# Repeated moving columns in two small TensorE products of a convolution and mixture-of-experts kernel, and another order of the logits products

## The chip, the cores and the metric

The kernel runs on one core of one Trainium2 chip. The metric is device time in microseconds. A profiled execution gives a span, from the first to the last instruction, and its own time beside it.

## The reference, cut to what matters

Tokens pass a causal convolution of seven taps per head and then a two-level mixture of experts: four groups of four experts, each token going to one expert, weighted by the product of two softmax values.

```python
# x: 8 x 2880 x 192, weight: 8 heads x 7 taps
w = exp(weight - max); w = w / (sum(w) + 1e-9)
out[b, s, h] = sum_k w[h, k] * x_pad[b, s + k, h]          # x for the experts, 23040 x 192
g_logits = x @ w_group                                     # 192 x 4
g_idx = argmax(g_logits); g_w = softmax(g_logits)[g_idx]
e_logits = x @ w_expert[g_idx]                             # 192 x 4 per group
e_idx = argmax(e_logits); e_w = softmax(e_logits)[e_idx]
y = maximum(x @ w1[g_idx, e_idx], 0) @ w2[g_idx, e_idx]    # 192 x 1024, 1024 x 192
out[token] = g_w * e_w * y
```

## The kernel before, in words

The 23040 tokens are cut into 192 blocks of 120 tokens, and the blocks into 18 units of 4, 8 or mostly 12 blocks. `unit` (L364) routes one unit. For each head a band matrix is multiplied with the tokens (L409), and ScalarE copies the result to `xc` (L418). TensorE turns the first 128 channels of a block into `ta` (L428) and the last 64 channels of two blocks into `tb` (L438). `logits` (L442) then multiplies them with the router weights for four blocks at a time: for each pair of blocks one product of `tb` with `wrb` (L448), which holds the weights of the last 64 channels for both blocks in 40 columns, and two products of `ta` with `wr` (L451), 20 columns each, added in PSUM. ScalarE copies 80 columns out to `lg` (L454). All these are f32. VectorE finds the expert and the weight of each token (L483 to L512), the unit's tokens with their weights are written to memory (L514), two small products count tokens per expert (L523, L524), and VectorE works out each token's place in its expert's list.

The list of a unit is itself made by a product. For each block VectorE writes two f16 matrices of zeros and ones, `ohl` with 128 columns and `ohv` with 32 (L549, L557), and TensorE multiplies them, one product per block, all added into 32 columns of one PSUM bank (L570). VectorE turns these into token numbers (L576, L578), and GpSimd scatters them to the table `idtab` (L581).

The experts come in slots of 256 tokens. GpSimd gathers the tokens (L653), TensorE turns them (L666, L667), `hidden` multiplies with the first weights (L684), ScalarE and VectorE split the result into two parts (L689, L690), and `back` multiplies with the second weights (L702, 384 columns; L706, 192 columns). VectorE and ScalarE add and scale the output (L753, L754), and GpSimd scatters it. The weights are loaded by SyncE (L602 to L606) and split on ScalarE and VectorE (L618 to L634); SyncE also loads the tokens for routing (L205, L207) and the lists (L976).

The first portion of slots needs the lists of the first five units, so these are routed first; the other units are routed in steps that are put between the expert products. The order of emission comes from tables of numbers (`UG`, `SK`, `KPRE`) and a rate, and the framework's scheduler then orders each engine's queue by its own estimate of durations. All PSUM comes from three pools of 2 KB banks; a bank holds 512 columns of f32.

Of the kernel before, what the change touches and what calls it, by code (L numbers as in the profile page):

```python
# [15 lines left out]
AF = mybir.ActivationFunctionType  # L16
# [4 lines left out]
P = 128  # L21
BT = 120
UB = 12
QB = 4
# [4 lines left out]
LH = 32  # L29
# [7 lines left out]
def conv_moe_kernel(  # L37
# [10 lines left out]
    nc = tc.nc  # L48
# [26 lines left out]
    NL = G + E  # L75
# [13 lines left out]
    for b in range(B):  # L89
        k = b * NB  # L90
# [84 lines left out]
    idtab = dram.tile([ROWS, 1], I32, name="idtab")  # L175
    tabd = dram.tile([NTAB, 4], I32, name="tabd")
    NVIEW = 12
    idviews = dram_disjoint_views(idtab[:, :], NVIEW)
    outviews = dram_disjoint_views(out, 8)
    nscat = [0]  # L180
# [48 lines left out]
    wr = const.tile([P, 2, NL], F32, name="wr")  # L229
# [16 lines left out]
    def clear_table():  # L246
# [12 lines left out]
        out=tri, in_=ones, pattern=[[1, P]], compare_op=ALU.is_gt, fill=0.0, base=0, channel_multiplier=-1,  # L259
# [12 lines left out]
    for nb in sorted({n for _, n in units}):  # L272
# [35 lines left out]
        out=sel, in_=ident.rearrange("p (e l) -> p e l", e=E), axis=AX.X, op=ALU.add)  # L308
    nc.gpsimd.iota(io[:, 0:1], pattern=[[0, 1]], base=0, channel_multiplier=1)
    nc.vector.tensor_scalar(  # L310
        out=io[:, 1:2], in0=io[:, 0:1], scalar1=LE - 1, scalar2=None, op0=ALU.bitwise_and)
# [6 lines left out]
    for g in range(NSK):  # L318
        nc.sync.dma_start(
            out=skew[0:R, g * HG:(g + 1) * HG],  # L320
            in_=bass.AP(wvd.tensor, wvd.offset + VL - KS - (BT - 1) + g * HG * VL, [[1, R], [VL, HG], [1, VW]]),
# [13 lines left out]
    for h in range(H):  # L335
        nc.scalar.activation(
            out=band[0:R, h], in_=skew[0:R, h, BT - 1::-1], func=AF.Exp, bias=wm[0:R, h:h + 1],
# [5 lines left out]
    wrb = const.tile([P, 2, NL], F32, name="wrb")  # L343
# [20 lines left out]
    def unit(u, pre=None):  # L364
# [4 lines left out]
        def bank(kind=None):  # L369
            if BK and kind and len(unit_banks) > 1:  # L370
                pool, nm = BKS[BK][kind]
                return pool.tile([P, 512], F32, name=nm)
            npool[0] += 1
            pool, nm = unit_banks[npool[0] % len(unit_banks)]
            return pool.tile([P, 512], F32, name=nm)
# [23 lines left out]
        for h in range(H):  # L399
# [8 lines left out]
            for i, (bb, xx) in enumerate(ops):  # L408
                nc.tensor.matmul(  # L409
                    out=ps[0:BT, 0:nb * HC], lhsT=bb[0:R, h, :], rhs=xx[0:R, :, cs],  # L410
                    start=i == 0, stop=i == len(ops) - 1,
# [8 lines left out]
        lg = rt.tile([P, UB, NL], F32, name="lg")[:, 0:nb]  # L420
# [21 lines left out]
        def logits(q):  # L442

            lgp = bank("l")
            ta, tb = parts[q]
            for i in range(QB // 2):
                o = lgp[0:BT, 2 * i * NL:2 * (i + 1) * NL]
                nc.tensor.matmul(  # L448
                    out=o, lhsT=tb[:, i * BT:(i + 1) * BT], rhs=wrb.rearrange("p a n -> p (a n)"), start=True, stop=False)
                for j in range(2):  # L450
                    nc.tensor.matmul(  # L451
                        out=o[:, j * NL:(j + 1) * NL], lhsT=ta[:, (2 * i + j) * BT:(2 * i + j + 1) * BT], rhs=wr[:, 0],
                        start=False, stop=j == 1)
            nc.scalar.activation(  # L454
                out=lg[0:BT, q * QB:(q + 1) * QB], in_=lgp[0:BT, 0:QB * NL].rearrange("p (b n) -> p b n", n=NL), func=AF.Copy)

        ga, gl, rest = gaps(u)
        events = {}
        for q in range(NQ):
            for k, f in ((ga, turn_a), (ga + 1, turn_b), (ga + gl, logits)):  # L460
                events.setdefault(k + 3 * q, []).append((f, q))
# [5 lines left out]
        Q = BT  # L467

        def bc(a, n):
            return a.unsqueeze(len(a.shape)).broadcast_to([*a.shape, n])  # L470
# [15 lines left out]
            out=sc, in0=dd, scalar=0.0, in1=prio[0:Q].unsqueeze(1).broadcast_to([Q, M, EG]),  # L486
# [9 lines left out]
            out=ohx[0:Q], in0=ohv[:, :, 1:NG, :].rearrange("p b g e -> p g e b"),  # L496
# [20 lines left out]
        while any(need <= u and pi not in idps for need, pi in needs.items()):  # L517
# [20 lines left out]
            out=posb[0:Q, 0], in0=pn, scalar1=-(LH - 1) / 2, scalar2=RND, op0=ALU.add, op1=ALU.add)  # L538
        nc.vector.scalar_tensor_tensor(
            out=posb[0:Q, 1], in0=posb[0:Q, 0], scalar=RND, in1=pn, op0=ALU.subtract, op1=ALU.subtract)  # L540

        halves = []
        for b0 in range(0, nb, HB2):
            n = min(HB2, nb - b0)
            ohl = pa.tile([P, HB2, P], F16, name="ohl", bufs=2)
            ohr = rt.tile([P, HB2, LH], F16, name="ohr", bufs=1)
            ohv5 = pa.tile([P, HB2, LH], F16, name="ohv", bufs=2)
            bs = slice(b0, b0 + n)
            nc.vector.tensor_tensor(  # L549
                out=ohl[0:Q, 0:n], in0=iop[0:Q].unsqueeze(1).broadcast_to([Q, n, P]), in1=bc(posb[0:Q, 0, bs], P),  # L550
# [3 lines left out]
                out=ohr[0:Q, 0:n], in0=ior[0:Q].unsqueeze(1).broadcast_to([Q, n, LH]), in1=bc(posb[0:Q, 1, bs], LH),  # L554
# [3 lines left out]
                out=ohv5[0:Q, 0:n], in0=ohr[0:Q, 0:n], in1=bc(vals[0:Q, bs], LH), op=ALU.mult)  # L558
# [8 lines left out]
        pl = bank("l")  # L567
        for b0, n, ohl, ohv5 in halves:
            for k in range(n):
                nc.tensor.matmul(  # L570
                    out=pl[:, 0:LH], lhsT=ohl[0:Q, k], rhs=ohv5[0:Q, k],
                    start=b0 + k == 0, stop=b0 + k == nb - 1,
                )
        lv5 = rt.tile([P, LH], F32, name="lv5", bufs=1)
# [2 lines left out]
            out=lv5, in0=pl[:, 0:LH], scalar1=0.0, scalar2=float(BIG), op0=ALU.is_equal, op1=ALU.mult)  # L577
        nc.vector.scalar_tensor_tensor(  # L578
            out=lsi, in0=pl[:, 0:LH], scalar=float(t0 - 1), in1=lv5, op0=ALU.add, op1=ALU.add)

        nc.gpsimd.indirect_dma_start(  # L581
            out=TABV, out_offset=bass.IndirectOffsetOnAxis(ap=rowi.bitcast(U32), axis=0),
            in_=lsi, in_offset=None,
# [334 lines left out]
    def step():  # L918

        if routed[0] < NU and len(live) < lead[1] and (not live or max(live, key=lambda a: a[0])[1] >= (lead[0] or SK[min(routed[0], len(SK)) - 1])):  # L920
            u = routed[0]
            live.append([u, 0, unit(u, xin0 if u == 0 else None)])
            routed[0] += 1
        if not live:
            return
        done[0] += 1
        cur = live.pop(0)
        cur[1] += 1
        try:
            next(cur[2])  # L930
            live.append(cur)
        except StopIteration:
            pass
# [84 lines left out]
    def tiles(i):  # L1018

        return 1 if plan[i][0] == "tail" and plan[i][1] >= NBIG else 2  # L1020
# [45 lines left out]
    k = 0  # L1066
    while routed[1] < portions[0][0]:
# [5 lines left out]
        for i in [i for i, kk in enumerate(KPRE) if kk == k]:  # L1073
            e, q = divmod(i, 5)
# [29 lines left out]
    for i, (pi, e, s) in enumerate(plan):  # L1104
# [4 lines left out]
        n = tiles(i)  # L1109
        oo = [po.tile([P, 512], F32, name="po") for _ in range(n)]  # L1110
        steps = NF // 2 if n == 2 else 2
        for f2 in range(steps):
# [27 lines left out]
            for q in range(f2, NF // 2, steps):  # L1140
                k = (q + 2) % 4
# [14 lines left out]
    with tc.If(nrare[0] != 0):  # L1156
        nover = nc.values_load(
            flagi[0:1, 0:1], min_val=0, max_val=1, skip_runtime_bounds_check_because=OOB_WHY)
        with tc.For_i(0, nover, 1):
            for u in range(NU):  # L1160
# [10 lines left out]
                    out=gi[:, 0], in0=gi[:, 1], scalar1=VS.bit_length() - 1, scalar2=None, op0=ALU.logical_shift_right)  # L1171
# [4 lines left out]
                    out=ee, in0=eoff[0:BT].unsqueeze(1).broadcast_to([BT, nb, E]),  # L1176
# [3 lines left out]
                    out=ee, in0=ee, in1=ends[0:BT, u].unsqueeze(1).broadcast_to([BT, nb, E]), op=ALU.mult)  # L1180
# [4 lines left out]
                for k in range(nb):  # L1185
                    nc.gpsimd.indirect_dma_start(
                        out=idtab[:, :], out_offset=bass.IndirectOffsetOnAxis(ap=gi[:, 0, k:k + 1].bitcast(U32), axis=0),
                        in_=idw[:, k:k + 1], in_offset=None,
# [48 lines left out]
```

## Time and profile before

| | |
|---|---|
| median of 3 runs | 1164.26 us (1162.6 to 1168.98) |
| the profiled execution | 1170.84 us, span 1169.0 us |
| mean granted TensorE clock | 0.977 of full speed |
| busy share of the span: PE, PEld, DVE, ACT, POOL | 95%, 92%, 69%, 59%, 43% |
| list products L570, in all | 192 |
| rows of logits products L451 and L448, in all | 384 and 192 |

PE is TensorE's matmul stream and PEld its weight loads, which overlap it; DVE is VectorE, ACT ScalarE, POOL GpSimd, SP SyncE. An f32 matmul stands in the trace as two rows, an f16 one as one. A busy time of PE counts modelled ends, so it is not a measure of useful columns; prices are better read from one start to the next. The granted clock is 1.00 or 0.50 in this trace, and it changes at edges 3.41 us apart.

### The profile page before, as it was taken

Reading aid. Unit: us, or ns where it says so; the run is one execution under the profiler, and the core shown is the slowest. Engines: PE = TensorE matmul, PEld = TensorE weight load, DVE = VectorE, ACT = ScalarE, POOL = GpSimd, SP = SyncE. Lnnn points to the kernel's source line nnn. Section 1 sums busy time; section 2 is a strip of 40 time slices with the busy share of each in tenths; the row PEclk is TensorE's granted clock in tenths of the full one; section 3 lists DMA queues with packets and bytes.
Section 4 is the critical chain, followed back from the end, with each engine's and each line's share of the span. In section 5 each row is a group of like instructions: output and inputs, shape, how many; then the busy total and the mean of one; then the engine's idle time right before and its main releaser. Section 6 shows DMA issues by size and latency. Waiting matters only on the chain.

```text
span 1169.0 us, 23803 instructions
## 1 busy us (share of the span) xinstructions
PE 1111.7 (95%) x8468; PEld 1079.3 (92%) x8468; DVE 804.5 (69%) x1668; ACT 690.1 (59%) x1374; POOL 498.2 (43%) x443
## 2 busy tenths in 40 slices
PE   5887999999999999999999999999999999999994
PEld 4766999998999999999999999999999999998984
DVE  4756788887877676666678565656565656688772
ACT  5544677657655555656554555555555656677772
POOL 2103234434434343434344444444444445578771
PEclk8879999999999999999999999999999999999997
DMA  8766699989775654546354574545454545599960
GB/s 228 217 182 178 173 213 230 226 203 268 217 194 143 165 156 118 143 116 170 95 162 95 155 203 128 142 128 141 130 141 128 140 118 167 146 243 266 248 160 19
DMA packets 167212, 195.63 MB, mean 167 GB/s; under 512 B 22500, under 2 KB 144333, under 8 KB 167086
## 3 DMA queue, kind: packets, MB, share of 16 engines
q1 hardware_dynamic: 125006, 140.41, 44.6%
q0 software_dynamic: 18752, 35.85, 10.5%
q10 hardware_dynamic: 23328, 17.80, 6.2%
q8 instruction: 67, 1.10, 0.4%
q14 instruction: 59, 0.48, 0.1%
HBM read 158.79 MB, written 36.58 MB: 167 GB/s over the span
## 4 chain that ended last, share of the span: by engine, by line
PE 79%; DVE 5%; DMA 4%; issue 3%; ACT 3%; another core or an unknown queue 0%; POOL 0%; POOLq 0%; ACTq 0%; DVEq 0%; SPq 0%
PE ph L684 33%; PE po L702 21%; PE po L706 10%; PE pm L409 3%; DMA xg<-xcd,idpt 3%; PE pm L451 2%; PE pm L666 2%; PE pm L667 2%; PE pm L428 1%; PE ph L719 1%; PE pm L448 1%; DVE hl L690 1%; DVE ohl L549 1%; DMA idtab<-lsi,rowi 1%; ACT cw L633 1%
## 5 line engine op out<-in xcount | busy, mean ns | idle before, releaser
L702 PE MATMUL po<-cw,hh 128*128 128x384 f32 x1424 | 443.4, 369 | 5.9 <-DVE ys L754 5.9
L684 PE MATMUL ph<-xa,ah 128*128 128x256 f32 x1424 | 390.2, 296 | 1.9 <-DVE xa L669 1.5
L757 POOL DMA_INDIRECT out<-ys,idp x160 | 167.8, 1049 | 447.4 <-DVE ys L754 348.8
L706 PE MATMUL po<-cw,hl 128*128 128x192 f32 x1424 | 357.3, 251 | 0.0
L690 DVE SCALAR_TENSOR_TENSOR hl<-ph,hh 128x512 fp32r<-128x512 f32 x356 | 241.2, 686 | 163.5 <-ACT hh L689 149.3
L689 ACT ACTIVATE hh<-ph 128x512 fp32r<-128x512 f32 x356 | 210.8, 594 | 205.8 <-PE ph L684 170.2
L702 PEld LDWEIGHTS po<-cw,hh 128*128 128x128 f32 x1424 | 268.6, 189 | 9.7 <-DVE ys L754 7.6
L684 PEld LDWEIGHTS ph<-xa,ah 128*128 128x128 f32 x1424 | 271.0, 190 | 5.0 <-DVE xa L669 1.6
L706 PEld LDWEIGHTS po<-cw,hl 128*128 128x128 f32 x1424 | 272.6, 191 | 1.5
L653 POOL DMA_INDIRECT xg<-xcd,idp x160 | 190.0, 1187 | 62.0 <-issue 29.6
L684 PE MATMUL ph<-xb,bh 128*128 128x256 f32 x712 | 201.9, 284 | 0.3 <-DVE xb L673 0.3
L684 PE MATMUL ph<-xb,bl 128*128 128x256 f32 x712 | 201.8, 283 | 0.0
L684 PE MATMUL ph<-xa,al 128*128 128x256 f32 x712 | 201.3, 283 | 0.0
L684 PEld LDWEIGHTS ph<-xa,al 128*128 128x128 f32 x712 | 136.5, 192 | 2.1
L684 PEld LDWEIGHTS ph<-xb,bl 128*128 128x128 f32 x712 | 136.7, 192 | 0.0
L684 PEld LDWEIGHTS ph<-xb,bh 128*128 128x128 f32 x712 | 136.2, 191 | 0.4 <-DVE xb L673 0.4
L634 DVE TENSOR_TENSOR cw<-rawc,cw 128x768 fp32r<-128x768 f32 x114 | 105.3, 953 | 18.3 <-ACT cw L633 13.7
L619 DVE TENSOR_TENSOR al<-raw,ah 128x1024 fp32r<-128x1024 f32 x57 | 70.5, 1238 | 38.8 <-ACT ah L618 21.6
L754 DVE SCALAR_TENSOR_TENSOR ys<-po,xg,ys 128x192 f32<-128x192 f32 x187 | 76.2, 416 | 23.2 <-ACT ys L753 18.1
L633 ACT ACTIVATE cw<-rawc 128x768 fp32r<-128x768 f32 x114 | 91.0, 837 | 1.8 <-DMA rawc<-in_moe_w 1.4
L672 ACT ACTIVATE xb<-pm 64x256 fp32r<-64x256 f32 x98 | 36.0, 367 | 93.4 <-DVE xa L669 86.2
L753 ACT ACTIVATE ys<-po,xg 128x192 f32<-128x192 f32 x187 | 75.8, 418 | 22.2 <-PE po L706 12.0
(216 smaller groups left out, 1561.0 us busy)
## 6 DMA issues: line engine op xcount, KB each, us to landing
rawc<-in_moe_w SPq DMA_DIRECT2D x114, 384.0 KB
raw<-in_moe_w SPq DMA_DIRECT2D x57, 512.0 KB
raw<-in_moe_w SPq DMA_DIRECT2D x114, 256.0 KB
xcd<-xc ACTq DMA_DIRECT2D x13, 1085.6 KB
xin<-in_x SPq DMA_DIRECT2D x7, 1134.0 KB
xc<-in_moe_w SPq DMA_DIRECT2D x18, 384.0 KB
xin<-in_x SPq DMA_DIRECT2D x6, 1039.5 KB
xin<-in_moe_w SPq DMA_DIRECT2D x9, 512.0 KB
```

The lines of the kernel that those rows point to most:

```text
L619: eng.get(k, nc.vector).tensor_tensor(out=al, in0=ra, in1=ah.bitcast(F32), op=ALU.subtract)
L633: pin(PINW, nc.scalar.activation(out=cw[:, fs, 0, :], in_=rc[k - 2], func=AF.Copy))
L634: eng.get(k, nc.vector).tensor_tensor(out=cw[:, fs, 1, :], in0=rc[k - 2], in1=cw[:, fs, 0, :].bitcast(F32), op=ALU.subtract,)
L653: nc.gpsimd.indirect_dma_start(out=xs[:, t, :], out_offset=None, in_=xcd[0:known, :], in_offset=bass.IndirectOffsetOnAxis(ap=ids[:, t, 0:1 ...
L684: nc.tensor.matmul(out=hp[:, j], lhsT=wgt[:, fs], rhs=xx, start=i == 0, stop=i == len(ops) - 1)
L689: nc.scalar.activation(out=hh, in_=hp, func=AF.Relu)
L690: nc.vector.scalar_tensor_tensor(out=hl, in0=hp, scalar=0.0, in1=hh.bitcast(F32), op0=ALU.max, op1=ALU.subtract,)
L702: nc.tensor.matmul(out=oo[t][:, 0:2 * D], lhsT=hh[:, j, ts], rhs=cw[:, f].rearrange("p a d -> p (a d)"), start=f == 0, stop=False,)
L706: nc.tensor.matmul(out=oo[t][:, 0:D], lhsT=hl[:, j, ts], rhs=cw[:, f, 0, :], start=False, stop=f == NF - 1,)
L753: nc.scalar.activation(out=ys[:, t, :], in_=oo[t][:, D:2 * D], func=AF.Copy, scale=g)
L754: nc.vector.scalar_tensor_tensor(out=ys[:, t, :], in0=oo[t][:, 0:D], scalar=g, in1=ys[:, t, :], op0=ALU.mult, op1=ALU.add,)
L757: nc.gpsimd.indirect_dma_start(out=outviews[nscat[0] % len(outviews)], out_offset=bass.IndirectOffsetOnAxis(ap=ids[:, t, 0:1].bitcast(U32) ...
```

## The change

Two constants are added, `REPL` = 5 and `REPO` = 6. In `logits`, the moving operand `wr` of a `ta` product is read five times over, so that 100 columns are streamed and written instead of 20; each block has its own 100 columns in the bank, 400 for four blocks, and only the first 20 of each are used. The two `ta` products of a pair now come first, and the product of `tb` follows as the third, writing only the 20 used columns of each of the two blocks (40 columns, as before). The first product of the pair starts the accumulation and the third ends it. ScalarE's copy reads the same 80 values, now 100 columns apart. In the list product the moving operand `ohv` is read six times over, 192 columns instead of 32, and VectorE still reads the first 32. Weight loads, the numbers of products and all other code are unchanged, though the scheduler orders some queues anew. Lines behind L177 move by two, behind the logits by up to four.

```diff
+    REPL = 5
+    REPO = 6
...
             for i in range(QB // 2):
-                o = lgp[0:BT, 2 * i * NL:2 * (i + 1) * NL]
-                nc.tensor.matmul(
-                    out=o, lhsT=tb[:, i * BT:(i + 1) * BT], rhs=wrb.rearrange("p a n -> p (a n)"), start=True, stop=False)
+                o = lgp[0:BT, 2 * i * REPL * NL:2 * (i + 1) * REPL * NL].rearrange("p (j n) -> p j n", j=2)
                 for j in range(2):
                     nc.tensor.matmul(
-                        out=o[:, j * NL:(j + 1) * NL], lhsT=ta[:, (2 * i + j) * BT:(2 * i + j + 1) * BT], rhs=wr[:, 0],
-                        start=False, stop=j == 1)
+                        out=o[:, j].rearrange("p (r n) -> p r n", n=NL), lhsT=ta[:, (2 * i + j) * BT:(2 * i + j + 1) * BT],
+                        rhs=wr[:, 0].unsqueeze(1).broadcast_to([P, REPL, NL]), start=j == 0, stop=False)
+                nc.tensor.matmul(
+                    out=o[:, :, 0:NL], lhsT=tb[:, i * BT:(i + 1) * BT], rhs=wrb, start=False, stop=True)
             nc.scalar.activation(
-                out=lg[0:BT, q * QB:(q + 1) * QB], in_=lgp[0:BT, 0:QB * NL].rearrange("p (b n) -> p b n", n=NL), func=AF.Copy)
+                out=lg[0:BT, q * QB:(q + 1) * QB],
+                in_=lgp[0:BT, 0:QB * REPL * NL].rearrange("p (b n) -> p b n", b=QB)[:, :, 0:NL], func=AF.Copy)
...
                 nc.tensor.matmul(
-                    out=pl[:, 0:LH], lhsT=ohl[0:Q, k], rhs=ohv5[0:Q, k],
+                    out=pl[:, 0:REPO * LH].rearrange("p (r n) -> p r n", r=REPO), lhsT=ohl[0:Q, k],
+                    rhs=ohv5[0:Q, k].unsqueeze(1).broadcast_to([Q, REPO, LH]),
                     start=b0 + k == 0, stop=b0 + k == nb - 1,
                 )
```

## The prediction

> **What bounds the kernel now.** I read the page first, then the busy time in five stretches, then the instructions in time where the three changed lines run, and last the granted clock around its drops.
>
> ```profile
> span 1169.0 us, 23803 instructions
> PEclk8879999999999999999999999999999999999997
> 16.32:116.00 99.68, 78.56 (x536) 67.25 (x535) 62.17 (x241) 51.44 (x142) 15.06 (x14) 0.83 0.76 203
> 116.00:640.00 524.00, 516.58 (x4054) 504.36 (x4055) 389.13 (x844) 314.12 (x636) 208.50 (x177) 0.99 0.65 171
> 640.00:1020.00 380.00, 380.00 (x2940) 379.48 (x2939) 241.85 (x387) 215.64 (x392) 168.80 (x157) 1.00 0.50 143
> ```
>
> After the start and the stretch name, the columns are busy us of PE, PEld, DVE, ACT and POOL, then the granted TensorE clock, the DMA share and GB/s. There are two stages that matter. Up to 116 us the first five units are routed before any expert can start: PE is busy 79% of that stretch at a mean clock of 0.83. From 116 us on TensorE is the bound: 516.58 of 524.00 us while the other units are routed between expert matmuls, and 380.00 of 380.00 us when routing is over. So TensorE time added between 116 and 640 us is paid nearly in full, and before 116 us only where it lies on the chain. The two changed products run only up to 621 us.
>
> **The list product.** These are the rows of one unit of 12 blocks and its neighbours (start, us, engine, line, operation, operands, shape, count).
>
> ```profile
> 132.28 0.25 PE L706 MATMUL po<-cw,hl 128*128 128x192 f32 x1
> 132.36 0.36 PE L702 MATMUL po<-cw,hh 128*128 128x384 f32 x1
> 132.56 0.25 PE L706 MATMUL po<-cw,hl 128*128 128x192 f32 x1
> 132.66 0.47 PE L570 MATMUL pm<-ohv,ohl 120*128 120x32 f16 x12
> 132.97 0.42 PE L702 MATMUL po<-cw,hh 128*128 128x384 f32 x1
> 133.23 0.25 PE L706 MATMUL po<-cw,hl 128*128 128x192 f32 x1
> 116.00:640.00 524.00, 5.19 (x132) 4.19 (x132) 0.99 0.65 171
> L570 PEld LDWEIGHTS <-ohl 120*128 120x128 f16 x192 | 7.5, 100 | 10.6 <-issue 4.6 <-DVE ohl L549 3.7 <-DVE ohv L557 1.4
> ```
>
> Durations overlap, so prices are read from start to start. Twelve 32-column products pass in 132.97 - 132.66 = 0.31 us, 0.026 us each. With 192 columns they cannot: an expert product that streams 192 columns holds the engine 0.08 us (132.28 to 132.36) to 0.09 (131.71 to 131.80 below). That is the upper bound. The lower one comes from the band product (next part): 288 columns in two passes cost 0.245 us a row, 0.245 / 576 = 0.43 ns a column, so 192 cost 0.082. I take 0.085, between them. Twelve are then 1.02 us instead of 0.31, 0.71 more. Something comes back: the L702 behind the list now takes 133.23 - 132.97 = 0.26 us, against 132.56 - 132.36 = 0.20 in the stream, because its weight load outlasts a 32-column product; a 192-column one covers those 0.06. That leaves 0.65 us a unit. The stretch row counts 132 list matmuls in the TensorE-bound stage, 11 units: **11 x 0.65 = +7.2 us** (bounds 6.8 with 0.082 and 7.8 with 0.09). Nothing hides it: TensorE is the engine that ends last there.
>
> The Trainium skill (TensorE: Matmul & The Clock Gate, LDWEIGHTS) prices a weight load at its columns / 1.2 GHz; by that rule 128 columns are 107 ns, the load would already be what the list product waits for, 192 columns would fit under it and this term would be zero. [...] The same page (Back-to-back issue gap) gives N / 2.4 + 2.5 ns, 82.5 ns for 192 columns, an estimate that would make this term 6.8.
>
> **The logits product.** At full clock, at half clock, and a product with 96 columns and two passes at half clock:
>
> ```profile
> 131.03 0.57 PE L451 MATMUL pm<-wr,ta 128*120 128x20 f32 x4
> 131.45 0.42 PE L702 MATMUL po<-cw,hh 128*128 128x384 f32 x1
> 131.71 0.25 PE L706 MATMUL po<-cw,hl 128*128 128x192 f32 x1
> 131.80 0.36 PE L702 MATMUL po<-cw,hh 128*128 128x384 f32 x1
> 71.71 0.97 PE L451 MATMUL pm<-wr,ta 128*120 128x20 f32 x4
> 72.51 1.29 PE L409 MATMUL ph<-xin,band 126*120 126x288 f32 x2
> 9.23 0.61 PE L409 MATMUL pm<-xin,band 126*120 126x96 f32 x2
> 9.63 0.61 PE L409 MATMUL po<-xin,band 126*120 126x96 f32 x2
> 78.46 0.65 PE L409 MATMUL ph<-xin,band 126*120 126x288 f32 x2
> 78.95 0.37 PE L438 MATMUL ph<-ident,xc 120*128 120x120 f32 x2
> ```
>
> An f32 product stands as two rows, each with its own load of 120 weight columns. Four 20-column rows take 131.45 - 131.03 = 0.42 us, 0.10 each at full clock; at half clock 72.51 - 71.71 = 0.80, 0.20 each. A 96-column f32 product of the same weight width takes 9.63 - 9.23 = 0.40 for its two rows, 0.20 each, the same price: both wait for the weight load, not for columns. At full clock 100 columns in two passes stream for 200 x 0.43 = 0.085 us (0.245 a row for 288: 78.95 - 78.46 = 0.49 for two), below 0.10. So the logits repeats cost **0**, covered by their own weight loads. Were that cover gone the price would be 0.10 + 0.085; the 96-column rows speak against it. Nothing is taken off for a gain either, since the loads stay. The order of the three products only swaps equal loads, and the copy out of PSUM still reads 80 elements.
>
> ```order
> L448 MATMUL po<-wrb,tb 120x40
> L451 MATMUL po<-wr,ta 120x20 x2
> L448 MATMUL po<-wrb,tb 120x40
> L451 MATMUL po<-wr,ta 120x20 x2
> L409 MATMUL ph<-xin,band 120x192 x2
> L409 MATMUL po<-xin,band 120x192 x2
> ```
>
> That was TensorE before, shortly ahead of the second unit's list product (wr and wrb are the router weights, ta and tb the turned tokens, band the convolution); this is the same place after the change:
>
> ```order
> L411 MATMUL ph<-xin,band 120x192 x2
> L451 MATMUL po<-wr,ta 120x100 x2
> L454 MATMUL po<-wrb,tb 120x2x20
> L451 MATMUL po<-wr,ta 120x100 x2
> L454 MATMUL po<-wrb,tb 120x2x20
> L411 MATMUL po<-xin,band 120x192 x2
> ```
>
> Two band products have moved ahead of the logits. Nearly every such move lies in the routing stage; behind it TensorE's order is the old one but for a few places.
>
> SyncE's queue moves there too. Before, with raw and rawc the weights and xin the tokens:
>
> ```order
> L602 DMA raw<-in_moe_w 128x1024
> L603 DMA raw<-in_moe_w 64x1024
> L207 DMA xin<-in_x 126x8x192
> L604 DMA raw<-in_moe_w 64x1024
> L606 DMA rawc<-in_moe_w 128x4x192 x2
> ```
>
> and after:
>
> ```order
> L606 DMA raw<-in_moe_w 128x1024
> L610 DMA rawc<-in_moe_w 128x4x192 x2
> L209 DMA xin<-in_x 126x8x192
> L607 DMA raw<-in_moe_w 64x1024
> L608 DMA raw<-in_moe_w 64x1024
> ```
>
> The two rawc loads now stand ahead of the sixth unit's tokens, and would hold them back if their buffer came free late; but that unit is not needed for the first portion, so I count 0 and keep 3 us to either side for all reordering before 116 us, less than the one wait of 3.94 us below.
>
> **The routing stage and the clock.** The chain has these list products and this wait, and the windows of the clock gate (edges from its changes, 3.41 us apart) read so:
>
> ```profile
> 70.44 0.20 PE pm L570 x2
> 83.42 0.30 PE pm L570 x6
> 98.54 0.20 PE pm L570 x8
> 101.03 3.94 another core or an unknown queue
> 67.52:70.93 3.41, 2.29 (x25) 2.00 (x24) 1.01 (x7) 1.08 (x4) 0.00 (x0) 1.00 0.99 273
> 70.93:77.76 6.83, 6.83 (x25) 5.63 (x25) 3.35 (x14) 3.01 (x9) 0.97 (x1) 0.50 0.30 74
> 91.41:94.82 3.41, 3.41 (x37) 3.38 (x35) 1.70 (x11) 2.49 (x7) 0.00 (x0) 1.00 0.92 149
> 94.82:98.24 3.42, 3.42 (x36) 3.42 (x35) 3.28 (x10) 2.24 (x7) 1.60 (x2) 1.00 0.81 218
> 617.06:620.47 3.41, 1.87 (x12) 1.66 (x13) 3.28 (x13) 3.36 (x7) 1.34 (x2) 1.00 0.04 14
> 620.47:623.89 3.42, 3.42 (x26) 3.33 (x26) 3.32 (x14) 0.65 (x2) 2.81 (x3) 0.50 0.65 184
> ```
>
> Sixteen list products on the chain, each 0.085 - 0.026 = 0.06 longer, are 0.95 us; a wait like the one at 101 us may swallow them (0), so I take **+0.6**.
>
> The clock fell to 0.50 at 620.47 behind a window in which TensorE was busy 1.87 of 3.41 us. It did not fall behind 91.41 to 94.82, which is full of logits with 20 columns, busy 3.41 us. So it follows idle time, not thin columns. The Trainium skill (TensorE: Matmul & The Clock Gate, Part 1) says that the gate goes by how busy the engine has recently been; this trace agrees, with those two windows.
>
> One drop can go: the window from 67.52 was busy 2.29 us and holds eight list products; 8 x 0.06 = 0.46 more makes 2.75. If the clock then stays up, 6.83 us of TensorE work at half clock, most of it on the chain, shrink by half, 3.4 us. The new order may also shift it, so I take half: **-1.7** (0 to -3.4). The other drops follow windows that are idle because data is missing.
>
> Sum: 7.2 + 0.6 - 1.7 = **+6.1 us**, bounds 6.8 + 0 - 3.4 = +3.4 and 7.8 + 1.0 - 0 = +8.8 before reordering. The profiled execution took 1170.84 us (its span is 1169.0), so 1176.9, a factor of 1.0052. The median of the runs shown is 1164.26, 6.6 lower; there the same factor gives **1170.3 us**.
>
> **The rivals.**
>
> ```profile
> 618.60 0.44 PE L702 MATMUL po<-cw,hh 128*128 128x384 f32 x1 [1.63 <-DVE ys L754]
> PE po L702 <- DVE ys L754: 5.9, 6, 1.6
> 116.00:640.00 524.00, 34.44 (x240) 30.00 (x240) 0.99 0.65 171
> sum 40.99, PE 32.66 PEld 27.09 DVE 24.78 ACT 15.55 POOL 8.60; mean PE 5.44 PEld 4.52 DVE 4.13 ACT 2.59 POOL 1.43
> ```
>
> A, the waits take it back. TensorE waits six times, 5.9 us in all, for VectorE to empty an output bank, as at 618.60; work added ahead of such a wait only shortens it. If all were ahead, 6.1 - 5.9 = +0.2, 1164.5. Against it: six waits, eleven units, and a list product only helps if it falls in the few us between VectorE's backlog and the wait.
>
> B, the logits are not covered. If each of the 240 rows in the TensorE-bound stage (last but one row above) cost 0.02 us more, because 0.085 is close to 0.10, that adds 4.8: 1170.3 + 4.8 = 1175. [...] Against it: the 96-column rows.
>
> C, the other side: the gate counts streamed columns, and thin products are what pulls the clock down. All half-clock stretches from 23 to 624 us would go; TensorE is busy 32.66 us in them (last row), half of that is 16.3, and 7.2 + 0.6 - 16.3 = -8.5 gives 1155.8. It decides from the point where most of them go: with under 13.6 us gained the result is not faster by 0.5%. In its favour, the Trainium skill (TensorE: Matmul & The Clock Gate, HAM oscillation) advises padding thin products to keep the engine warm. Against it: 91.41 to 98.24, thin columns at full clock, and most of these stretches follow true waits.
>
> **How the numbers follow.** A measurement of this kernel can tell about 0.5%, 5.8 us, from no change. Chances: forecast 0.62, A 0.15, B 0.12, C 0.11. The forecast lies just above the bound; its own range, 1164.26 + 3.4 - 3 to 1164.26 + 8.8 + 3, 1164.7 to 1176.1, has a bit over half above: 0.33 slower, 0.29 same. With B slower 0.45, with A same 0.44, with C faster 0.11. The range leaves out C and the far end of B: 1162.5 (A, with 2 us of reordering) to 1178.5 (B, with 3).
>
> **What would show it.** Twelve list products in about 1.0 us instead of 0.31 and TensorE's stretch from 116 us to the end of routing longer by about 7; logits rows still 0.10 apart; half clock still behind idle windows, with or without the stretch at 71 us. It is wrong if list products still start 0.026 apart, if logits rows start 0.12 or more apart, or if half-clock time before 116 us is nearly gone.

## The result, and the profile after

The changed kernel is slower. Its median is 1178.32 us (1174.0 to 1183.85, 6 runs) against 1165.38 for the kernel before (1160.61 to 1171.18, 6 runs); the ratio is 1.0109, with a 95% interval of 1.0078 to 1.014, so about 12.7 us were lost. The profiled execution is the one of 1178.32 us. The profiled execution of before, 1170.84 us, lies at the upper end of its runs, so the two traces differ by only 7.5 us: they show where time goes, and the ratio says how much.

The page of the changed kernel, and the same stretches as before (start and stretch in us, busy us of PE, PEld, DVE, ACT, POOL, granted clock, DMA share, GB/s):

```profile
span 1176.6 us, 23810 instructions
PEclk9969899999999999999999999999999999999998
16.32:116.00 99.68, 80.04 (x538) 70.47 (x536) 62.32 (x240) 52.27 (x145) 15.56 (x14) 0.88 0.77 205
116.00:640.00 524.00, 513.33 (x3982) 501.57 (x3982) 382.68 (x833) 307.54 (x624) 200.94 (x172) 0.99 0.63 170
640.00:1020.00 380.00, 380.00 (x2946) 380.00 (x2947) 241.89 (x388) 213.98 (x390) 169.10 (x158) 1.00 0.50 139
```

TensorE is nearly as busy as before between 116 and 640 us (513.33 us instead of 516.58), but it gets through 3982 matmul rows there instead of 4054. One reason is seen in the instructions of one unit's list and logits:

```profile
137.27 0.25 PE L710 MATMUL po<-cw,hl 128*128 128x192 f32 x1
137.36 1.17 PE L573 MATMUL pm<-ohv,ohl 120*128 120x192 f16 x12
138.31 0.42 PE L706 MATMUL po<-cw,hh 128*128 128x384 f32 x1
138.57 0.25 PE L710 MATMUL po<-cw,hl 128*128 128x192 f32 x1
138.65 0.36 PE L706 MATMUL po<-cw,hh 128*128 128x384 f32 x1
138.85 0.25 PE L710 MATMUL po<-cw,hl 128*128 128x192 f32 x1
138.94 0.58 PE L451 MATMUL pm<-wr,ta 128*120 128x100 f32 x4
139.35 0.32 PE L454 MATMUL pm<-wrb,tb 128*120 128x40 f32 x2
139.51 0.64 PE L451 MATMUL pm<-wr,ta 128*120 128x100 f32 x4
139.99 0.32 PE L454 MATMUL pm<-wrb,tb 128*120 128x40 f32 x2
140.14 0.36 PE L688 MATMUL ph<-xa,ah 128*128 128x256 f32 x1
```

Twelve list products take 138.31 - 137.36 = 0.95 us instead of 0.31. Twelve logits rows take 140.14 - 138.94 = 1.20 us. In the kernel before, with L448 first, the twelve rows are these, and the next expert product starts at 131.45:

```profile
130.25 0.32 PE L448 MATMUL pm<-wrb,tb 128*120 128x40 f32 x2
130.40 0.57 PE L451 MATMUL pm<-wr,ta 128*120 128x20 f32 x4
130.82 0.38 PE L448 MATMUL pm<-wrb,tb 128*120 128x40 f32 x2
131.03 0.57 PE L451 MATMUL pm<-wr,ta 128*120 128x20 f32 x4
```

That is 1.20 us as well: 100 columns cost what 20 did.

The other new thing stands where routing hands over to the experts. First TensorE, then VectorE, then GpSimd there:

```profile
113.96 1.17 PE L573 MATMUL pm<-ohv,ohl 120*128 120x192 f16 x12
120.60 0.63 PE L440 MATMUL pm<-ident,xc 120*128 120x120 f32 x2 [5.47 <-DVE lsi L582]
```

```profile
114.02 0.16 DVE L566 TENSOR_REDUCE rows<-rows 128x1 f32<-128x16 f32 x1
119.96 0.16 DVE L567 TENSOR_TENSOR rowi<-rows,goff 128x1 int32<-128x1 f32 x1 [5.77 <-DMA idtab<-lsi,rowi]
120.04 0.18 DVE L580 TENSOR_SCALAR lv<-pm 128x32 f32<-128x32 f32 x1
120.26 0.19 DVE L582 SCALAR_TENSOR_TENSOR lsi<-pm,lv 128x32 int32<-128x32 f32 x1
120.48 0.75 DVE L677 TENSOR_TENSOR xb<-pm,xb 64x256 fp32r<-64x256 f32 x2
```

```profile
100.47 1.20 POOL L657 DMA_INDIRECT xg<-xcd,idp  x1 [10.31 <-DMA idp<-idtab]
...
109.98 1.62 POOL L657 DMA_INDIRECT xg<-xcd,idp  x1 [0.30 <-issue]
111.91 1.63 POOL L585 DMA_INDIRECT idtab<-lsi,rowi  x1 [0.30 <-DVE pick L511]
```

VectorE writes the row numbers (`rowi`) of one unit's list, for which there are two buffers, and waits until the scatter of the unit before, still in flight, has read its own. That scatter went out at 111.91, behind eight gathers, and the wait for it ended at 119.96. (With two buffers one would expect a wait for the scatter before that one, which went out at 89.19; why it is the latest is not shown.) While VectorE waits, everything behind it in its queue waits: the token numbers `lsi`, which empty the PSUM bank that TensorE's next operation (L440) needs, and the two splits `xb` on which the next expert products hang. TensorE stands for 5.47 us. In the kernel before the same place reads:

```profile
115.53 0.42 DVE L673 TENSOR_TENSOR xb<-pm,xb 64x256 fp32r<-64x256 f32 x1
115.98 0.19 DVE L576 TENSOR_SCALAR lv<-pm 128x32 f32<-128x32 f32 x1
116.08 0.16 DVE L563 TENSOR_REDUCE rows<-rows 128x1 f32<-128x16 f32 x1
116.20 0.19 DVE L578 SCALAR_TENSOR_TENSOR lsi<-pm,lv 128x32 int32<-128x32 f32 x1
116.31 0.15 DVE L564 TENSOR_TENSOR rowi<-rows,goff 128x1 int32<-128x1 f32 x1
```

There `xb` goes first and `rowi` last, when the scatter is over. An earlier `rowi` does wait in the kernel before too, for 2.04 us; its critical chain has this scatter and this wait:

```profile
62.50 7.32 DMA idtab<-lsi,rowi
69.84 0.16 DVE rowi L564
```

The scheduler, which orders the queues by estimated durations, was told of longer list products, and `rowi` now stands ahead. So the theory to test is: about 7 us are the list product's columns, about 5 us the new place of `rowi`, and the logits repeats are free. The rivals: the logits repeats have a share; the wait at the handover is harmless, since something else would be waited for; the columns are absorbed in waits and all is queue order.

### The profile page after: what moved, and what is told of

Its sections match the earlier page's. It is cut to its first block, busy times and chain, and to the rows that moved or that the text cites. A ratio compares the mean times of both kernels' runs of the same rounds, so it can differ in the third digit from the quotient of the medians.

```text
span 1176.6 us, 23810 instructions
## 1 busy us (share of the span) xinstructions
PE 1118.6 (95%) x8468; PEld 1088.7 (93%) x8468; DVE 805.3 (68%) x1668; ACT 689.8 (59%) x1374; POOL 495.7 (42%) x443
## 4 chain that ended last, share of the span: by engine, by line
PE 76%; DMA 7%; DVE 5%; issue 2%; ACT 2%; POOL 1%; SPq 0%; POOLq 0%; DVEq 0%; ACTq 0%
PE ph L688 32%; PE po L706 20%; PE po L710 9%; DMA xg<-xcd,idpt 4%; PE pm L411 3%; PE pm L451 2%; DMA idtab<-lsi,rowi 2%; PE pm L670 1%; PE pm L671 1%; PE pm L430 1%; PE pm L573 1%; DVE hl L694 1%; PE pm L454 1%; DVE cw L638 1%; POOL out L761 1%
```

## The experiments

All ratios are to the kernel before. Its median over the runs beside them was 1166.8 to 1167.0 us.

**The list product alone.** The logits go back to 20 columns, in the new order.

```diff
-    REPL = 5
+    REPL = 1
```

> Only the list product is repeated (six times, 192 columns); the logits products keep 20 columns but stand in the new order. Theory (the loss is the list product's columns, about 7 us on TensorE, plus about 5 us where VectorE's new queue order lets the row-number operation wait for a scatter at the handover to the experts; the logits repeats are free): this kernel has the same queue order at the handover as the full change and loses nearly all of it, ratio to the kernel before 1.009 to 1.012. Rival (the logits repeats carry a share, their streams not being covered by the weight loads): ratio 1.004 to 1.007.

Measured: 1.0134 (1.0103 to 1.0166), median 1184.7 us. All of the loss is there without the logits repeats, and more than the 1.009 to 1.012 that was expected. Why it is more stays open; that this kernel is worse than the full change is not shown, since the intervals overlap.

**The logits alone.**

```diff
-    REPO = 6
+    REPO = 1
```

> Only the logits products are repeated (five times, 100 columns) and stand in the new order; the list product keeps 32 columns, and VectorE's queue at the handover is as in the kernel before. Theory: ratio 0.997 to 1.003, logits rows still about 0.10 us apart at full clock, no long wait of the row-number operation ahead of the second token-split. Rival (logits not covered): ratio 1.004 to 1.007, rows 0.12 us apart or more.

Measured: 1.0006 (0.9984 to 1.0027). The rows of its trace, from the first logits product to the next expert product:

```profile
128.14 0.58 PE L451 MATMUL pm<-wr,ta 128*120 128x100 f32 x4
128.55 0.32 PE L454 MATMUL pm<-wrb,tb 128*120 128x40 f32 x2
128.71 0.64 PE L451 MATMUL pm<-wr,ta 128*120 128x100 f32 x4
129.18 0.32 PE L454 MATMUL pm<-wrb,tb 128*120 128x40 f32 x2
129.34 0.42 PE L706 MATMUL po<-cw,hh 128*128 128x384 f32 x1
```

Again 1.20 us for twelve rows. The logits repeats and their new order cost nothing that can be measured, and gain nothing. The first rival falls.

**The full change without the wait for a scatter.** Four buffers instead of two for what the scatter reads, wherever these tiles are made (four places, of which two are shown), so that a scatter in flight need not be waited for:

```diff
-        rowi = rt.tile([P, 1], I32, name="rowi")
+        rowi = rt.tile([P, 1], I32, name="rowi", bufs=4)
...
-        lsi = rt.tile([P, LH], I32, name="lsi")
+        lsi = rt.tile([P, LH], I32, name="lsi", bufs=4)
```

> The full change with four buffers instead of two for the row numbers and the token numbers of a list, so that writing them need not wait until an earlier scatter has read them; every queue's order is that of the full change. Theory: the wait of 5.8 us at the handover goes, TensorE's wait of 5.5 us with it, and the time falls by 4 to 6 us, ratio to the kernel before 1.005 to 1.008. Rival (the first expert products are bound by something else anyway, so the wait is replaced by another): within 1 us of the full change, ratio 1.010 to 1.012.

Measured: 1.0063 (1.0038 to 1.0087), median 1174.28 us, some 4 us below the full change, as the theory had it, though the two intervals overlap. TensorE's, ScalarE's, GpSimd's and SyncE's queues have the order of the full change; in VectorE's one `rowi` of an earlier unit stands six places sooner, which was not expected. The wait at the handover is nearly gone in the trace, though in this execution one of 5.62 us for a gather stands ahead of it, so this pair of runs alone would not settle the second rival.

**The kernel before with the same four buffers.**

> The kernel before with the same four buffers, nothing else; queue orders are unchanged. Theory: the waits for scatters are short here (2.0 us at 70 us, 8.8 us at 117 us where the operation stands behind the urgent ones), so the time falls by 0 to 3 us, ratio 0.997 to 1.000. Rival (that wait bounds the routing stage in every kernel, changed or not): a fall of 5 us or more, ratio below 0.996.

The 8.8 us that the expectation names at 117 us are GpSimd's wait for `rowi`, not a wait for a scatter. Measured: 0.9982 (0.9956 to 1.0008). No gain that can be told from none. A gain of up to 5 us lies within the interval, but the wait of TensorE at the handover is not in the trace of the kernel before, so nothing here says that it bounds that kernel; it came with the change.

**Only the later units.** The list product is repeated only in the 11 units whose lists come behind the handover.

```diff
+        reps = REPO if u > 6 else 1
...
-                    out=pl[:, 0:REPO * LH].rearrange("p (r n) -> p r n", r=REPO), lhsT=ohl[0:Q, k],
-                    rhs=ohv5[0:Q, k].unsqueeze(1).broadcast_to([Q, REPO, LH]),
+                    out=pl[:, 0:reps * LH].rearrange("p (r n) -> p r n", r=reps), lhsT=ohl[0:Q, k],
+                    rhs=ohv5[0:Q, k].unsqueeze(1).broadcast_to([Q, reps, LH]),
```

> The list product is repeated six times only in the units behind the seventh (ten or eleven units that run between expert products); the logits stand and repeat as in the full change. VectorE's queue at the handover is that of the kernel before (row numbers behind the first token split). Theory: the streamed columns alone, 11 units x 0.65 = 7 us, no handover wait: ratio 1.005 to 1.008. Rival (most of the loss comes from queue order, the columns are absorbed in waits): ratio 0.999 to 1.003.

Measured: 1.0053 (1.0033 to 1.0074), 6.2 us. That is the price of the columns where TensorE is the bound. Its row of `rowi`, and TensorE's only wait above 0.5 us behind it:

```profile
117.26 0.16 DVE L567 TENSOR_TENSOR rowi<-rows,goff 128x1 int32<-128x1 f32 x1 [5.27 <-DMA idtab<-lsi,rowi]
117.64 0.42 PE L430 MATMUL pm<-ident,xc 120*128 120x120 f32 x2 [1.01 <-DVE ends L532]
```

VectorE waits 5.27 us here too, but the first `xb` was ahead of it, and TensorE has expert products to go on with. Only 1.01 us of TensorE's time is lost behind it, for `ends`, which stands behind `rowi` in VectorE's queue. The wait costs by its place in the queue, not by its length alone. The third rival falls.

**Only the first six units**, with two buffers and then with four:

```diff
+        reps = REPO if u < 6 else 1
```

> The list product is repeated only in the first six units (48 products, nearly all in the routing stage); the logits as in the full change. VectorE's queue at the handover has row numbers and token numbers ahead of the second token split, as in the full change. Theory: some 2 us of columns on the routing stage's chain at most and 4 to 6 us of handover wait: ratio 1.003 to 1.007, with a wait of the row-number operation for a scatter above 4 us in the trace. Rival (the handover order costs nothing): ratio 0.999 to 1.002.

> The same as the run with the first six units, with four buffers instead of two for row numbers and token numbers; TensorE's, ScalarE's and SyncE's queues have the same order. Theory: the handover wait is gone and the time falls by 4 us or more against that run, ratio to the kernel before 0.998 to 1.002. Rival (another wait takes its place): within 1.5 us of that run.

Measured: 1.0049 (1.0027 to 1.0071) with two buffers and 0.9992 (0.9968 to 1.0015) with four; the medians are 1172.79 and 1165.75. TensorE's waits around the handover, first with two buffers:

```profile
113.57 0.62 PE L689 MATMUL ph<-xa,ah 128*128 128x256 f32 x3 [2.35 <-DVE xa L674]
120.81 0.63 PE L440 MATMUL pm<-ident,xc 120*128 120x120 f32 x2 [6.31 <-DVE lsi L583]
```

and with four:

```profile
111.90 0.33 PE L671 MATMUL pm<-ident,xg 128*128 128x128 f32 x1 [2.38 <-DMA xg<-xcd,idp]
115.55 0.63 PE L440 MATMUL pm<-ident,xc 120*128 120x120 f32 x2 [0.60 <-DVE lsi L583]
```

6.31 us become 0.60, and the kernel gets its 0.0057, 6.6 us, back; the two intervals do not overlap. The queue orders differ by one operation of an earlier unit, a `rowi`. With two buffers that one waits as well, 4.10 us at 73.62, and with four it does not. This earlier wait explains at most 0.8 us: from the scatter ahead of it to the first gather the two traces take 35.5 us (65.44 to 100.91) and 34.7 (66.30 to 100.97). From the first gather to the first output, at 139.33 and 133.39, they take 38.4 and 32.4. So 6.0 us are lost at the handover itself, and the second rival falls. The clock is down for longer there, too:

```profile
116.07:126.31 10.24, 5.50 (x26) 5.43 (x27) 2.39 (x6) 1.82 (x4) 1.00 (x1) 0.50 0.69 201
112.73:119.55 6.82, 6.22 (x41) 5.95 (x40) 3.04 (x13) 2.47 (x7) 0.52 (x1) 0.50 0.95 245
```

With two buffers (first row) the granted clock at the handover is 0.50 for 10.24 us, with four for 6.82.

The 48 wider products of the routing stage cost nothing by themselves that can be told from none: with the wait gone, the ratio is 0.9992 (0.9968 to 1.0015), and the kernel before with four buffers had 0.9982.

**Twelve repeats instead of six**, with four buffers.

```diff
-    REPO = 6
+    REPO = 12
```

> The full change with four buffers, and the list product repeated twelve times (384 columns) instead of six. Theory: each product takes about 0.165 us instead of 0.085, so 11 units x 12 x 0.08 = 10.6 us more than the run with six repeats and four buffers, and up to 1.5 us more on the routing stage's chain: ratio to the kernel before 1.015 to 1.018. Rival (the loss of the repeats is a fixed price, whatever their number): ratio 1.005 to 1.009.

Measured: 1.0167 (1.0139 to 1.0195), against 1.0063 with six: 12 us more for 192 columns more. In its trace:

```profile
140.60 0.25 PE L710 MATMUL po<-cw,hl 128*128 128x192 f32 x1
140.69 2.13 PE L573 MATMUL pm<-ohv,ohl 120*128 120x384 f16 x12
142.52 0.47 PE L706 MATMUL po<-cw,hh 128*128 128x384 f32 x1
```

Twelve products take 1.83 us, 0.88 more than with six repeats; eleven units make 9.7 of the 12 us. The price goes by the columns. Whether the rest is the routing stage's was not tried; in this trace the first gather goes out at 105.97 us, with six repeats at 99.22, but these are two single executions.

## Why the prediction was right or wrong

The loss is twice the forecast: 12.7 us instead of 6.1. It went the way that was thought likeliest, though only by 0.45 against 0.44 for no change. That the time lies inside the range, by 0.2 us, is luck. The forecast's own range ended at 1176.1; the upper end of 1178.5 came from rival B, which the runs disproved, and B's sum is 1175 + 3 = 1178, so 1178.5 does not come out of it. The columns were forecast rightly, and the other half of the loss is a wait that the prediction did not see.

- The list product in the stage that TensorE bounds: +7.2 forecast; 0.95 - 0.31 = 0.64 us a unit, 7.0 in all, by the trace, and 6.2 us (3.9 to 8.6) by the run with the later units alone. Right, though by two errors that cancel: a product takes 0.079 us, not 0.085, and the 0.06 us that the next expert product was to give back did not come (138.57 - 138.31 = 0.26, as before). The Trainium skill's rule for weight loads (TensorE: Matmul & The Clock Gate, LDWEIGHTS), under which the term would be zero, does not hold for these f16 loads: twelve products with a load of 128 columns each start within 0.31 us, and the wider ones cost 0.64 us a unit more. What sets the 0.026 us of a 32-column product, its load or something else, no run here tells.
- The logits: 0 forecast, 1.20 us for twelve rows in both kernels, 1.0006. Right, and rival B, which wanted 0.02 us a row, is out.
- The routing stage's columns: +0.6 forecast, nothing measured (0.9992 with the first six units and four buffers). Inside the bound that let a wait swallow them, and 0.6 us is too little for these runs to tell from zero.
- The clock: -1.7 forecast, not seen. In the changed kernel's trace the stretch from 74.1 to 80.9 us is still at half clock, in the place of the one at 71 us that was to vanish. All stretches at half clock between the first full-clock one and the last one, at the kernel's end, sum to 41 us in the profile before and 34 in the one after, but 34 as well in the run of the kernel before with four buffers; the other traces lie between 27 and 48. No gain of time goes with it. At the handover it went the other way: half clock from 115.05 to 125.29 us, where the kernel before has 115.30 to 118.72. (The estimate itself has a slip: 8 x 0.06 is 0.48, not 0.46.) Rival C, the other side, is out: with 384 columns instead of 32 there were still 27 us at half clock, and the kernel was slower. Rival A, absorption in waits, is out by the run with the later units alone.
- The step that failed is the one on order: "I count 0 and keep 3 us to either side for all reordering before 116 us". It looked at TensorE's and SyncE's queues, and at the wait of 3.94 us that stood in the trace. It did not look at VectorE's queue at the handover, where `rowi` had moved ahead of the first `xb` split and of the token numbers. The trace of before held the warning: the scatter issued at 62.50 us kept a `rowi` waiting until 69.84, and the `rowi` at the handover was harmless because it stood last. With the wait at 6.6 us by the pair of runs with the first six units, 6.2 + 6.6 = 12.8 is the loss that was measured; each of the two terms is uncertain by some 2.5 us, so that they meet it so closely is in part chance.

What stays open is why executions of one kernel differ by 13 us here (1160.5 to 1173.9 for the kernel before). Traces show waits for gathers of 2 to 6 us at the handover in some executions and none in others, but no run isolates them.

## What to carry to other kernels

How far a product can be widened for nothing has to be read per product. Here an f32 row with 120 weight columns took 0.10 us with 20 moving columns and with 100; an f16 product with 128 weight columns took 0.026 us with 32 and 0.079 with 192. Where between 32 and 192 the price sets in was not measured. Where a scheduler orders the queues, a change of a duration on one engine can move an operation that waits on another; look in every in-order queue at what now stands behind an operation that waits for a DMA. In this kernel a second pair of buffers for what a scatter reads took the wait away, in both kernels that had it at the handover.

## What the runs showed of the hardware that was not expected

Twelve f16 loads of 128 weight columns each show about 100 ns in the trace and yet follow one another every 0.026 us with 32 columns streamed, 0.079 with 192 and 0.153 (1.83 / 12) with 384. Scatters of one unit's list, 128 rows, let a waiting `rowi` go between 5.3 us after their issue (65.47 to 70.77, list product alone) and 9.2 us (64.66 to 73.90, the changed kernel), with no gathers ahead of them. The one behind eight gathers took 8.1 us (111.91 to 119.96). The gathers delayed its issue, for its list had been written at 105.1; that they lengthen it is not shown.
